# First MLP in five passes of 256 tokens and two of 512, in place of five of 288 and two of 432

## The chip, the cores and the metric

The program runs on one core of one Trainium2 chip, from one launch. The metric is the device time of one execution in microseconds. Each time that the kernel has is the median of several executions; beside them there is one execution under the hardware profiler, from which every row below is read.

## What is computed

Pooled attention over 4 batches, 8 heads, 576 positions of 64 channels, and then two MLPs over the 2304 tokens that come out of it, 512 channels wide. All inputs and outputs are float32.

```python
k_p = k.reshape(B, H, Sp, pool, D).mean(axis=3)          # pool = 8, Sp = 72
v_p = v.reshape(B, H, Sp, pool, D).mean(axis=3)
scores = scale * np.matmul(q, k_p.transpose(0, 1, 3, 2))
attn = softmax(scores)                                    # over the 72 pooled keys
x = np.matmul(attn, v_p) -> [2304, 512]

rms = np.sqrt(np.mean(x * x, axis=-1, keepdims=True) + 1e-06)
xn = x / rms * rms_g
g = xn @ w_gate                                           # 512 x 1536
silu = g * (1.0 / (1.0 + np.exp(-g)))
x = silu * (xn @ w_val) @ w_out                           # 1536 x 512

h = x @ w_in                                              # 512 x 2048
out = (h * (1.0 / (1.0 + np.exp(-h)))) @ w_out2           # 2048 x 512
```

The change concerns the first MLP alone, and how its tokens are cut.

## The kernel before

**Tokens.** Attention makes tokens in eight chunks of 288 (`CH`), two per batch; a chunk stands in the tile `xraw` as 128 partitions by 4 blocks of channels (`KT`) by 288 tokens. The first MLP runs over these chunks in passes. Passes 0 to 4 take chunks 0 to 4, one each (288 tokens). Chunks 5 to 7 are written to DRAM (`x_spill`) and read again for two wide passes of 432 tokens (`WB`). The name `CB` is the number of narrow passes.

**One step of a pass** treats one of the 12 blocks of 128 hidden channels (f = 0 to 11): `gate` and `val` multiply the pass's tokens by a block of w_gate and w_val, `down1` multiplies the product by a block of w_out into four accumulators. Each of the three is 12 matmuls on TensorE, since float32 is split in a high and a low part and three of the four products are taken (`mm3`, lines 261 to 263): 36 matmuls a step, whose moving operand is the pass's tokens, so 288 or 432 columns. Between them ScalarE does a tanh (L637), VectorE two products (L639, L655) and the split of the result in its two parts (ACT L241 or DVE L243 for the copy, L248 for the difference). The wide passes do the same in `gatew`, `valw`, `downw`.

**Weights** come from DRAM as float64 and are turned into two float32 parts by seven instructions a block (`w_block`: L175, L182 or L190, L194, and the two parts at L243/L241 and L248), mostly on VectorE. There are 36 such blocks. They are not all there when the first passes run: pass 0 does only f = 0 to 2 and pass 1 only f = 0 to 5 (`CUT`); what they leave out is done after pass 4, in two further passes that read the tokens back (`x_back`), pass 0 with 9 steps and pass 1 with 6. Pass 2 is the first with all 12 steps, and the first that needs every block. Steps before the end of pass 2: 3 + 6 + 12 = 21; after it 12 + 12 + 9 + 6 = 39; all times 36 matmuls are 2160 narrow matmuls. The wide passes have 2 x 12 x 36 = 864.

**Tokens for a pass** are split by `x_split` into the tiles `xT0` to `xT3`, one per block of channels, with one buffer each: a copy and a difference per tile, which may begin only when the last pass has read that tile for the last time.

**The second MLP** (line 786, `up2` and `down2`) is two levels of seven products in place of eight, in three blocks of 768 tokens, with moving operands of 384 and of 256 columns. Its code is not changed.

**The order** of all this is written out by hand as four strings of step names (`start`, `pair`, `last`, `second`), such as `2G0` for the next part of gate of step 0 of pass 2, `B17` for the next part of weight block 17, `:v` or `:g` or `:a` for the engine. `play` calls the parts in that order, and each engine takes its instructions in the order in which they were recorded. There is no other scheduler.

Of the kernel before, what the change touches and what calls it, by code (L numbers as in the profile page):

```python
# [22 lines left out]
def tile_pooled_attention_then_two_mlps(  # L23
# [25 lines left out]
    P = 128  # L49
# [21 lines left out]
    WB = (NCH - CB) * CH // 2  # L71
    WP = 448
# [201 lines left out]
    xraw = att.tile([P, KT, CH], F32, name="xraw")  # L274

# [304 lines left out]

    def x_spill(c, j):
        if c in x_d:
            nc.sync.dma_start(out=x_d[c][j], in_=xraw[:, j, :])
        else:
            for p, a, z in wide(c):
                n = p * WB - (c - CB) * CH
                nc.sync.dma_start(out=xw_d[p][j][:, a:z], in_=xraw[:, j, a + n:z + n])
        yield

    def wide(c):  # L590

        n = (c - CB) * CH
        for p in range(2):
            a, z = max(n, p * WB), min(n + CH, (p + 1) * WB)
            if a < z:
                yield p, a - p * WB, z - p * WB

    def steps(c):
# [7 lines left out]
            "r": lambda i: stats(c), "n": lambda i: normalise(c), "y": x_split,  # L606
# [16 lines left out]
    def gate(i, f):  # L623
        w = w_t["gate", f]
        pg = psum.tile([P, 512], F32, tag="up", bufs=2, name="pg")[:, :CH]
        for j in range(KT):
            m = slice(j * P, (j + 1) * P)
            mm3(pg, w[:, 0, m], w[:, 1, m], xT[j][:, 0, :CH], xT[j][:, 1, :CH], j == 0, j == KT - 1)
        yield
        if i == 0:  # L630

            g = early_x[:, f % 2 * CH:(f % 2 + 1) * CH]
            nc.vector.tensor_tensor(out=g, in0=pg, in1=early_x[:, 2 * CH:3 * CH], op=ALU.mult)
            yield
            pg = g
        th_t[i, f] = th = p1.tile([P, CH], F32, tag="ev", bufs=2, name="th")
# [4 lines left out]
        if i == 0:  # L641
            combine("g", th, th, early_x[:, 2 * CH:3 * CH], ALU.mult)
            yield

    def val(i, f):
        w = w_t["val", f]
        ps = psum.tile([P, 512], F32, tag="up", bufs=2, name="pv")[:, :CH]
        for j in range(KT):
            m = slice(j * P, (j + 1) * P)
            mm3(ps, w[:, 0, m], w[:, 1, m], xT[j][:, 0, :CH], xT[j][:, 1, :CH], j == 0, j == KT - 1)  # L650
# [6 lines left out]
        hT[i, f] = t = p1.tile([P, 2, CH], F32R, tag="hT", bufs=2, name="hT")  # L657
        yield from split(t[:, 0, :], t[:, 1, :], h, "v" if 2 <= i < NCH - 1 else "a", "v")

    def down1(i, f):  # L660
# [13 lines left out]
    def part_load(i):  # L674
        t = [slot() for _ in range(2)]
        part_t[i] = t = [t[e // 2][:, e % 2 * CH:(e % 2 + 1) * CH] for e in range(KT)]
# [4 lines left out]
    def y1_store(i, e):  # L681
# [4 lines left out]
        else:  # L686
            y = tmp("y")
# [7 lines left out]
    def x_back(i, j):  # L695
# [676 lines left out]
```

## Time and profile before

| what | value |
|---|---|
| median of 3 runs | 907.18 us (906.56 to 907.39) |
| the profiled execution | 906.69 us |
| its span, first to last instruction | 904.9 us |
| TensorE busy | 897.5 us |
| VectorE, ScalarE, GpSimd busy | 629.6, 541.0, 382.8 us |
| granted TensorE clock, mean | 0.998 |

A matmul's busy time in the profile reaches from its start to the modelled end of its results, and matmuls overlap; a busy TensorE is not one at its best rate. The rate is read from the starts of matmuls that follow each other. Busy times of the other engines are unions of their instructions' times.

Seen from TensorE, the span has five stretches: attention alone with filler matmuls up to 42 us; passes 0, 1 and 2 with attention for the next chunks and the weight blocks up to 166 us; passes 3 and 4 and the two left-over passes up to 384 us; the wide passes up to 556 us; and the second MLP. The windows in the rows below are cut close to these.

### The profile page before, as it was taken

How to read it: one execution, taken by the hardware profiler on the slowest of the kernel's cores; microseconds unless marked ns; L12 is line 12 of the kernel's file. 1: busy time of each engine (PE TensorE's matmuls, PEld its weight loads, DVE VectorE, ACT ScalarE, POOL GpSimd, SP SyncE). 2: the span in 40 equal slices, each digit the busy share in tenths (PEclk: the TensorE clock that was granted, in tenths of full speed). 3: DMA queues.
4: the chain of work that ended last, by engine and by line, in shares of the span. 5: the costliest groups of instructions: out<-in, count | busy, mean ns of one | idle time of the engine just before them, and what ended most of it. 6: DMA issues, size and time to landing. Idle time of an engine off the chain costs nothing.

```text
span 904.9 us, 17610 instructions
## 1 busy us (share of the span) xinstructions
PE 897.5 (99%) x6262; PEld 880.5 (97%) x6262; DVE 629.6 (70%) x1255; ACT 541.0 (60%) x1452; POOL 382.8 (42%) x488
## 2 busy tenths in 40 slices
PE   8999999999999999999999999999999999999998
PEld 8789999999999999999999999999999999999998
DVE  7899998665454836443477789757976589766675
ACT  6789876373354714344444556777657776577653
POOL 6646434372217521100028666980048810399100
PEclk9999999999999999999999999999999999999999
DMA  8765632351314322244468886266852678623485
GB/s 264 235 201 189 205 108 78 94 176 43 92 42 123 102 66 61 86 145 150 151 207 277 271 277 203 72 232 217 269 191 70 211 213 274 209 73 141 139 263 205
DMA packets 85260, 149.81 MB, mean 166 GB/s; under 512 B 8627, under 2 KB 53812, under 8 KB 85172
## 3 DMA queue, kind: packets, MB, share of 16 engines
q1 hardware_dynamic: 85172, 148.68, 50.8%
q8 instruction: 49, 0.80, 0.4%
q14 instruction: 39, 0.32, 0.1%
HBM read 116.21 MB, written 32.44 MB: 164 GB/s over the span
## 4 chain that ended last, share of the span: by engine, by line
PE 96%; POOL 1%; DMA 1%; issue 1%; ACT 1%; DVE 0%; SPq 0%; ACTq 0%; POOLq 0%
PE P L786 38%; PE pv L261 6%; PE pv L263 6%; PE pv L262 6%; PE pg L261 6%; PE acc L261 6%; PE acc L262 6%; PE pg L262 6%; PE acc L263 6%; PE pg L263 6%; PE sc L418 2%; PE pT L469 1%; DMA early_raw<-in_moe_w_gate_dram 1%; PE idle L331 1%; PE pv L504 1%
## 5 line engine op out<-in xcount | busy, mean ns | idle before, releaser
L786 PE MATMUL P<-xP,in 128*128 128x384 f32 x1008 | 176.5, 336 | 0.0
L786 PEld LDWEIGHTS P<-xP,in 128*128 128x128 f32 x1008 | 175.0, 188 | 0.1
L786 PE MATMUL P<-out,hc 128*128 128x256 f32 x1512 | 172.8, 276 | 0.0
L786 PEld LDWEIGHTS P<-out,hc 128*128 128x128 f32 x1512 | 172.6, 188 | 0.0
L248 POOL TENSOR_TENSOR in<-in,in 128x256 fp32r<-128x256 f32 x96 | 80.3, 845 | 112.1 <-DMA out_dram<-o 48.2
L241 ACT ACTIVATE hc<-h 128x384 fp32r<-128x384 f32 x144 | 73.6, 524 | 42.6 <-PE P L786 36.3
L248 DVE TENSOR_TENSOR hc<-h,hc 128x384 fp32r<-128x384 f32 x144 | 79.9, 581 | 18.5 <-ACT hc L241 15.1
L261 PE MATMUL pg<-xT,w_gate 128*128 128x288 f32 x240 | 72.6, 303 | 0.3 <-DVE hT L248 0.3
L261 PE MATMUL pv<-xT,w_val 128*128 128x288 f32 x240 | 72.8, 303 | 0.0
L261 PE MATMUL acc<-hT,w_out 128*128 128x288 f32 x240 | 72.2, 301 | 0.0
L263 PE MATMUL pv<-xT,w_val 128*128 128x288 f32 x240 | 70.9, 295 | 0.3 <-POOL w_val L248 0.3
L262 PE MATMUL acc<-hT,w_out 128*128 128x288 f32 x240 | 71.0, 296 | 0.0
L262 PE MATMUL pg<-xT,w_gate 128*128 128x288 f32 x240 | 70.9, 295 | 0.0
L262 PE MATMUL pv<-xT,w_val 128*128 128x288 f32 x240 | 70.8, 295 | 0.0
L263 PE MATMUL pg<-xT,w_gate 128*128 128x288 f32 x240 | 70.8, 295 | 0.0
L263 PE MATMUL acc<-hT,w_out 128*128 128x288 f32 x240 | 70.8, 295 | 0.0
L637 ACT ACTIVATE th<-pg 128x288 f32<-128x288 f32 x57 | 23.3, 409 | 70.0 <-PE pg L263 69.0
L436 ACT ACTIVATE pr<-sc,mx 96x72 f32<-96x72 f32 x192 | 57.9, 316 | 11.7 <-DVE mx L429 10.9
L248 POOL TENSOR_TENSOR in<-sums,in 128x256 fp32r<-128x256 f32 x72 | 58.5, 820 | 5.8 <-ACT in L241 5.5
L639 DVE SCALAR_TENSOR_TENSOR th<-th,pg 128x288 f32<-128x288 f32 x57 | 25.7, 451 | 36.8 <-ACT th L637 36.5
L263 PEld LDWEIGHTS pv<-xT,w_val 128*128 128x128 f32 x240 | 45.3, 189 | 0.6 <-POOL w_val L248 0.6
L261 PEld LDWEIGHTS pv<-xT,w_val 128*128 128x128 f32 x240 | 45.1, 188 | 0.7 <-ACT kbd L241 0.4
(236 smaller groups left out, 2324.1 us busy)
## 6 DMA issues: line engine op xcount, KB each, us to landing
out<-out SPq DMA_DIRECT2D x84, 512.0 KB, 4.6
out<-out2s SPq DMA_DIRECT2D x56, 256.0 KB, 2.9
in<-in SPq DMA_DIRECT2D x24, 512.0 KB, 3.7
raw<-in_moe_w_out_dram SPq DMA_DIRECT2D x18, 512.0 KB, 4.3
raw<-in_moe_w_in_dram SPq DMA_DIRECT2D x16, 512.0 KB, 3.7
early_raw<-in_moe_w_gate_dram SPq DMA_DIRECT2D x10, 512.0 KB, 4.4
early_raw<-in_moe_w_val_dram SPq DMA_DIRECT2D x10, 512.0 KB, 4.9
early_raw<-in_moe_w_out_dram SPq DMA_DIRECT2D x10, 512.0 KB
```

The source lines that it names most:

```text
L241: nc.scalar.activation(out=out, in_=in_, func=AF.Copy, scale=1.0 if scale is None else scale)
L248: ENGINES[engine[0] or usual].tensor_tensor(out=out, in0=in0, in1=in1, op=op)
L261: nc.tensor.matmul(ps, lhsT=whi, rhs=xhi, start=first, stop=False)
L262: nc.tensor.matmul(ps, lhsT=whi, rhs=xlo, start=False, stop=False)
L263: nc.tensor.matmul(ps, lhsT=wlo, rhs=xhi, start=False, stop=last)
L331: nc.tensor.matmul(idle[0][:, :P], lhsT=zero, rhs=zero, start=True, stop=True, skip_group_check=True)
L418: nc.tensor.matmul(ps[:TT, a * 2 * SP:(a + 1) * 2 * SP], lhsT=qT[:, a * TT:(a + 1) * TT], rhs=kbd[:, j, :], start=True, stop=True,)
L436: nc.scalar.activation(out=pr[:, a, e], in_=s4[:, a, e], func=AF.Exp, bias=mx[:, a, e:e + 1], accum_out=sm[:, a, e],)
L469: nc.tensor.transpose(ps[:n, a * TT:(a + 1) * TT], src, ident[:TT, :TT])
L637: nc.scalar.activation(out=th, in_=pg, func=AF.Tanh, scale=0.5)
L639: nc.vector.scalar_tensor_tensor(out=th, in0=th, scalar=1.0, in1=pg, op0=ALU.add, op1=ALU.mult)
L786: nc.tensor.matmul(ps, lhsT=a, rhs=b, start=first and n == 0, stop=n == 2, skip_group_check=True)
```

## The change

The narrow passes take 256 tokens (`TP`) in place of 288, still five of them, and the wide passes 512 in place of 432: 5 x 256 + 2 x 512 = 2304 as 5 x 288 + 2 x 432 was. Chunks of attention stay at 288 tokens. What chunk c has left over after pass c, 32 (c + 1) tokens, is copied by GpSimd into a new tile `left` and opens pass c + 1, so that pass c takes 32 c tokens from `left` and 256 - 32 c from `xraw`. `x_split` therefore has two copies and two differences per tile in passes 1 to 4 where it had one of each. For chunk 0 the left-over tokens are also scaled by GpSimd. Of chunk 4, 160 tokens go to the wide passes. The tiles in DRAM, the results and the loads for the second MLP are cut at the new places. Some tiles change their memory: the wide passes' `thw` stands where `hT` stood, `fr` has five places in place of six, `y1_wide` has one `e` buffer in place of two. The number of matmuls is the same, 140 filler matmuls included. The order strings are new throughout, for all engines.

```diff
-    WB = (NCH - CB) * CH // 2
-    WP = 448
+    TP = 256
+    WB = (NT - CB * TP) // 2
...
+    left = att.tile([P, KT, P], F32, name="left")
...
             nc.sync.dma_start(out=rs_d[c], in_=rs[:1])
             yield
+            t = kept(c)
+            combine("g", t, t, rs[:, None, TP:].to_broadcast([P, KT, CH - TP]), ALU.mult)
+            yield
             return
...
+    def kept(c):
+
+        n = (c + 1) * (CH - TP)
+        return left[:, :, P - n:] if c == 0 else left[:, :, :n]
+
     def x_spill(c, j):
         if c in x_d:
-            nc.sync.dma_start(out=x_d[c][j], in_=xraw[:, j, :])
+            n = c * (CH - TP)
+            if n:
+                nc.sync.dma_start(out=x_d[c][j][:, :n], in_=kept(c - 1)[:, j, :])
+            nc.sync.dma_start(out=x_d[c][j][:, n:], in_=xraw[:, j, :TP - n])
...
-    def x_split(j):
-        xT[j] = t = p1.tile([P, 2, CH], F32R, tag=f"xT{j}", bufs=1, name=f"xT{j}")
-        yield from split(t[:, 0, :], t[:, 1, :], xraw[:, j, :], "a", "v")
+    def x_tile(j):
+        if len(xT) == 2 and j not in xT:
+            p1.tile([P, 32], F32, tag="shift", bufs=1, name="shift")
+        xT[j] = t = p1.tile([P, 2, TP], F32R, tag=f"xT{j}", bufs=1, name=f"xT{j}")
+        return t
+
+    def x_split(c, j):
+        t = x_tile(j)
+        n = c * (CH - TP)
+        if n:
+            yield from split(t[:, 0, :n], t[:, 1, :n], kept(c - 1)[:, j, :], "a", "v")
+        yield from split(t[:, 0, n:], t[:, 1, n:], xraw[:, j, :TP - n], "a", "v")
+        if c < CB - 1:
+            copy("g", kept(c)[:, j, :], xraw[:, j, TP - n:])
+            yield
...
-        pg = psum.tile([P, 512], F32, tag="up", bufs=2, name="pg")[:, :CH]
+        pg = psum.tile([P, 512], F32, tag="up", bufs=2, name="pg")[:, :TP]
...
-            k = n_fr[0] % 6
+            k = n_fr[0] % 5
...
-        xw[j] = t = pw[0].tile([P, 2, WP], F32R, tag=f"x{j}", bufs=1, name=f"xw{j}")[:, :, :WB]
+        xw[j] = t = pw[0].tile([P, 2, WB], F32R, tag=f"x{j}", bufs=1, name=f"xw{j}")
...
-        thw[f] = th = pw[0].tile([P, WB], F32, tag="e", bufs=2, name="thw")
+        thw[f] = th = p1.tile([P, WB], F32, tag="hT", bufs=2, name="thw")
...
-        if p == 1 and e < 2:
-            y = pw[0].tile([P, WB], F32, tag="e", bufs=2, name="yw")
+        if e % 2:
+            y = pw[0].tile([P, WB], F32, tag="e", bufs=1, name="yw")
...
-        "B35 3n0 3y1:g 3y0 2H11 3n0 2H11:a 2D10 3y0:g 3y2 2H11 3y1 3n0 3y3 2D11 2D11 3y2 3y3 2D11 2D11"
+        "B35 3y1 3y1 2H11 2H11:a 3n0 3n0 3y1:g 2H11 3y0 3y0 3y0 2D10 3y0:g 3n0 3n0 3y2 3y2 3y2 3y1 3y3 3y3 3y0 "
+        "3y3 2D11 2D11 3y2 3y3 3y3 2D11 2D11"
```

How the instructions stand at the end of pass 2 and the start of pass 3. Names carry a number that tells buffers apart; `w_out11` is the last weight block, `hT` the split product for the last `down1`, `xT` the tokens of pass 3. VectorE before:

```order
L243 CAST w_out11_2322<-raw_2237 128x512
L248 TENSOR_TENSOR xraw_162<-xraw_162,rs_2304 128x288
L655 TENSOR_TENSOR pv_2308<-th_2299,pv_2308 128x288
...
L248 TENSOR_TENSOR hT_2332<-pv_2308,hT_2332 128x288
L248 TENSOR_TENSOR xT1_2326<-xraw_162,xT1_2326 128x288
...
L248 TENSOR_TENSOR xT2_2347<-xraw_162,xT2_2347 128x288
L248 TENSOR_TENSOR xT3_2352<-xraw_162,xT3_2352 128x288
L245 TENSOR_SCALAR y_2368<-acc1_1665 128x288
```

VectorE after, at the same place:

```order
L244 CAST w_out11_2355<-raw_2268 128x512
L249 TENSOR_TENSOR xT1_2358<-left_162,xT1_2358 128x96
L674 TENSOR_TENSOR pv_2333<-th_2346,pv_2333 128x256
L249 TENSOR_TENSOR xraw_161<-xraw_161,rs_2351 128x288 x2
L249 TENSOR_TENSOR hT_2362<-pv_2333,hT_2362 128x256
L249 TENSOR_TENSOR xT0_2368<-left_162,xT0_2368 128x96
L249 TENSOR_TENSOR xraw_161<-xraw_161,rs_2351 128x288 x2
L249 TENSOR_TENSOR xT2_2387<-left_162,xT2_2387 128x96
L249 TENSOR_TENSOR xT1_2358<-xraw_161,xT1_2358 128x160
L249 TENSOR_TENSOR xT3_2392<-left_162,xT3_2392 128x96
L249 TENSOR_TENSOR xT2_2387<-xraw_161,xT2_2387 128x160
L249 TENSOR_TENSOR xT3_2392<-xraw_161,xT3_2392 128x160
```

Four differences from `left` have come in between; the weight block and `hT` stand where they stood, and the operations of the step itself are 32 columns narrower.

GpSimd at the same place, before:

```order
L550 TENSOR_TENSOR ms_2261<-ms_2261,mhalf_122 96x3
L248 TENSOR_TENSOR w_val11_2281<-raw_2196,w_val11_2281 128x512
L248 TENSOR_TENSOR w_out11_2322<-raw_2237,w_out11_2322 128x512
L243 CAST xT1_2326<-xraw_162 128x288
L248 TENSOR_TENSOR xT0_2328<-xraw_162,xT0_2328 128x288
L338 TENSOR_TENSOR kv_2370<-kv_2370 96x256
```

And after:

```order
L552 TENSOR_TENSOR ms_2295<-ms_2295,mhalf_121 96x3
L249 TENSOR_TENSOR w_val11_2315<-raw_2230,w_val11_2315 128x512
L249 TENSOR_TENSOR w_out11_2355<-raw_2268,w_out11_2355 128x512
L244 CAST xT1_2358<-xraw_161 128x160
L249 TENSOR_TENSOR xT0_2368<-xraw_161,xT0_2368 128x160
L244 COPY left_162<-xraw_161 128x128 x2
L340 TENSOR_TENSOR kv_2414<-kv_2414 96x256
```

The copies of what chunk 3 leaves over stand behind the last weight blocks and ahead of the sums of v.

## Rows read from the trace of the kernel before

**Rows 1.** Page, parts 1 and 4: busy time; the chain that ended last.
```profile
PE 897.5 (99%) x6262; PEld 880.5 (97%) x6262; DVE 629.6 (70%) x1255; ACT 541.0 (60%) x1452; POOL 382.8 (42%) x488
...
PE 96%; POOL 1%; DMA 1%; issue 1%; ACT 1%; DVE 0%; SPq 0%; ACTq 0%; POOLq 0%
```

**Rows 2.** Windows: stretch, its length, then each engine's busy us and instructions.
```profile
core 0: us, PE busy (x) PEld busy (x) DVE busy (x) ACT busy (x) POOL busy (x), PEclk, DMA share, GB/s
...
40.00:105.00 65.00, 64.26 (x475) 60.49 (x474) 63.76 (x147) 58.10 (x170) 32.66 (x42) 1.00 0.61 192
105.00:165.00 60.00, 59.99 (x460) 59.64 (x459) 52.96 (x115) 40.35 (x90) 25.57 (x23) 1.00 0.33 107
165.00:384.00 219.00, 218.64 (x1688) 217.97 (x1688) 119.34 (x287) 98.29 (x366) 77.40 (x121) 1.00 0.29 87
384.00:552.00 168.00, 168.00 (x863) 161.11 (x862) 105.37 (x176) 83.95 (x163) 57.94 (x65) 1.00 0.64 214
```

**Rows 3.** Timeline of TensorE, narrow passes: start, us, engine, line, form.
```profile
379.81 0.29 PE L262 MATMUL pv<-xT,w_val 128*128 128x288 f32 x1
...
384.32 0.29 PE L263 MATMUL acc<-hT,w_out 128*128 128x288 f32 x1
```

**Rows 4.** The same view, wide passes and second MLP.
```profile
399.66 0.36 PE L261 MATMUL pv<-xw,w_val 128*128 128x432 f32 x1
...
403.57 0.36 PE L263 MATMUL acc<-hw,w_out 128*128 128x432 f32 x1
...
639.78 4.47 PE L786 MATMUL P<-out,hc 128*128 128x256 f32 x38
```

**Rows 5.** Page, part 5: a matmul of 256 columns, busy us, mean ns.
```profile
L786 PE MATMUL P<-out,hc 128*128 128x256 f32 x1512 | 172.8, 276 | 0.0
```

**Rows 6.** Timeline of VectorE, GpSimd and TensorE at the end of pass 2.
```profile
161.84 0.41 DVE L243 CAST w_out<-raw 128x512 fp32r<-128x512 f32 x1
163.05 0.46 DVE L655 TENSOR_TENSOR pv<-th,pv 128x288 f32<-128x288 f32 x1 [0.44 <-PE pv L263]
164.06 0.46 DVE L248 TENSOR_TENSOR hT<-pv,hT 128x288 fp32r<-128x288 f32 x1 [0.19 <-ACT hT L241]
...
162.33 1.32 POOL L248 TENSOR_TENSOR w_out<-raw,w_out 128x512 fp32r<-128x512 f32 x1 [2.26 <-DVE w_out L243]
...
164.44 0.29 PE L261 MATMUL acc<-hT,w_out 128*128 128x288 f32 x1
...
166.14 0.30 PE L261 MATMUL pg<-xT,w_gate 128*128 128x288 f32 x1
```

**Rows 7.** VectorE's waits, 40 to 105 us: waiter <- releaser: us, times, longest.
```profile
DVE th L639 <- ACT th L637: 0.6, 1, 0.6
DVE early_x L633 <- PE pg L263: 0.3, 1, 0.3
```

**Rows 8.** VectorE's waits, 105 to 165 us, the four longest.
```profile
DVE pv L655 <- PE pv L263: 1.9, 3, 0.8
DVE pT L243 <- PE pT L469: 1.4, 1, 1.4
DVE th L639 <- ACT th L637: 0.9, 1, 0.9
DVE raw L175 <- DMA raw<-in_moe_w_val_dram: 0.8, 1, 0.8
```

**Rows 9.** Groups by form, VectorE and GpSimd: count, busy us, mean ns of one.
```profile
L1049 DVE TENSOR_TENSOR o<-P,s 128x512 f32<-128x512 f32 x3 | 2.1, 687 | 0.4 <-PE P L786 0.4
L1049 DVE TENSOR_TENSOR o<-P,s 128x256 f32<-128x256 f32 x3 | 1.2, 415 | 0.0
L248 DVE TENSOR_TENSOR vt<-vs,vt 32x64 fp32r<-32x64 f32 x1 | 0.2, 215 | 0.0
L248 DVE TENSOR_TENSOR vbd<-vs,vbd 64x64 fp32r<-64x64 f32 x8 | 2.3, 289 | 0.2
L243 POOL COPY rest<-pr 96x144 f32<-96x144 f32 x15 | 6.7, 452 | 25.8 <-DVE pr L248 25.5
```

More of the change, by code (lines that the diff above doesn't have):

```diff
@@ L579, in normalise @@
             yield
+    def kept(c):
+        n = (c + 1) * (CH - TP)
+        return left[:, :, P - n:] if c == 0 else left[:, :, :n]
     def x_spill(c, j):
         if c in x_d:
-            nc.sync.dma_start(out=x_d[c][j], in_=xraw[:, j, :])
-        else:
-            for p, a, z in wide(c):
-                n = p * WB - (c - CB) * CH
-                nc.sync.dma_start(out=xw_d[p][j][:, a:z], in_=xraw[:, j, a + n:z + n])
-        yield
[L590 to L596, printed above, removed]
+            n = c * (CH - TP)
+            if n:
+                nc.sync.dma_start(out=x_d[c][j][:, :n], in_=kept(c - 1)[:, j, :])
+            nc.sync.dma_start(out=x_d[c][j][:, n:], in_=xraw[:, j, :TP - n])
+        else:
+            n = c * CH - CB * TP
+            for p in range(2):
+                a, z = max(n, p * WB), min(n + CH, (p + 1) * WB)
+                if a < z:
+                    nc.sync.dma_start(out=xw_d[p][j][:, a - p * WB:z - p * WB], in_=xraw[:, j, a - n:z - n])
+        yield
     def steps(c):
@@ L675, in part_load @@
         t = [slot() for _ in range(2)]
-        part_t[i] = t = [t[e // 2][:, e % 2 * CH:(e % 2 + 1) * CH] for e in range(KT)]
+        part_t[i] = t = [t[e // 2][:, e % 2 * TP:(e % 2 + 1) * TP] for e in range(KT)]
         for e in range(KT):
@@ L722, in fr @@
         if not late:
-            k = n_fr[0] % 6
+            k = n_fr[0] % 5
             n_fr[0] += 1
-            return p1.tile(
-                [P, 2, 256], F32R, tag="hT" if k > 3 else f"xT{k}", bufs=2 if k > 3 else 1, name=name
-            )
+            pool, tag = (pw[0], "e") if k > 3 else (p1, f"xT{k}")
+            return pool.tile([P, 2, 256], F32R, tag=tag, bufs=1, name=name)
         n_late[0] += 1
@@ L850, in y1_wide @@
         yield
-        for c in range(CB, NCH):
-            for q, a, z in wide(c):
-                if q == p:
-                    n = p * WB - (c - CB) * CH
-                    nc.sync.dma_start(out=y1_d[c][:, e, a + n:z + n], in_=y[:, a:z])
+        nc.sync.dma_start(out=y1_d[CB + p][:, e, :], in_=y)
         yield
@@ L864, in x2_steps @@
         t0 = c * N2
-        for n in range(t0 // CH, (t0 + N2 - 1) // CH + 1):
-            a, z = max(t0, n * CH), min(t0 + N2, (n + 1) * CH)
-            nc.sync.dma_start(out=x2raw[:, :, a - t0:z - t0], in_=y1_d[n][:, :, a - n * CH:z - n * CH])
+        for (n, m), y1 in zip(parts, y1_d):
+            a, z = max(t0, n), min(t0 + N2, n + m)
+            if a < z:
+                nc.sync.dma_start(out=x2raw[:, :, a - t0:z - t0], in_=y1[:, :, a - n:z - n])
         yield
```

39 lines of the change are left out of this document (20 added, 19 removed), and 324 rows, old and new, of tables (last, pair, second, start).

## The prediction

> **What bounds the kernel now.** I read the page first: TensorE is busy for 897.5 us of the span of 904.9 us, and the chain that ended last lies on it for 96% [rows 1]. So the first question is what a matmul costs, and the second where TensorE is only just fed. For the cost I took the starts of matmuls that follow each other without a break. In the narrow passes 35 matmuls start between 379.81 and 384.32 us [rows 3]: 4.51 / 34 = 132.6 ns each for 288 columns. In the wide passes 21 start between 399.66 and 403.57 us: 3.91 / 20 = 195.5 ns for 432 columns. In the second MLP 38 matmuls of 256 columns take 4.47 us together [rows 4]; less the 276 ns of the last one [rows 5], 4.19 / 37 = 113.4 ns. At the higher of the clock's two levels, 2.4 GHz, which the granted clock of 1.00 is [rows 2], columns alone would be 106.7, 120.0 and 180.0 ns. So 256 columns carry 6.7 ns on top, 288 carry 12.6 and 432 carry 15.5: between 256 and 288 there is a step of 5.9 ns beyond the 13.3 ns of the columns.
>
> Then I read the windows by stretch, to see who else is full [rows 2]. From 40 to 105 us VectorE is busy 63.76 of 65 us, from 105 to 165 us 52.96 of 60: it has 1.24 + 7.04 = 8.3 us to spare in 125. From 165 us on it is busy 54 to 63% and TensorE alone sets the pace. The end of pass 2 shows what the first stretch means [rows 6]: the high part of the last weight block is made at 161.84 us on VectorE, its low part ends at 162.33 + 1.32 = 163.65 us on GpSimd, the last hT ends at 164.06 + 0.46 = 164.52 us, and TensorE begins the `down1` that needs both at 164.44. Nothing lies ready there. Up to the start of pass 3 at 166.14 us, TensorE and VectorE end together.
>
> **The matmuls.** The change takes 32 columns off 2160 matmuls and adds 80 to 864; the sum of columns is the same, so only the step counts. A narrow one goes from 132.6 to 113.4 ns, if 256 columns cost in the first MLP what they cost in the second: 19.2 ns less. For 512 columns there is no row. Twice the row of 256 is 226.8 ns; 195.5 plus 80 columns at 2.4 GHz (33.3 ns) is 228.8; with one more step of 5.9 ns it is 234.7. I take 228.8, since 432 columns already carry more than 288 do and 2 x 256 would want a lower overhead than the nearest row has; both ends stay for the range. The wide passes then cost 864 x 33.3 ns = +28.8 us (27.0 to 33.9). VectorE and ScalarE get longer there too, but VectorE was busy 105.37 of 168 us [rows 2], and TensorE gets more time than they do, so I cost that at nothing. The cover would be gone if a step's products took longer than its 36 matmuls, now 8.2 us.
>
> The narrow side falls in two parts. After pass 2 there are 39 steps of 36, 1404 matmuls: 1404 x 19.2 = -27.0 us. VectorE has 99.7 us to spare of 219 there, ScalarE and GpSimd more, so all of it should reach the end. Before that there are 21 steps, 756 matmuls, which would be -14.5 us, if TensorE were alone.
>
> **The first 166 us.** It is not alone. I went through VectorE's instructions up to the last weight block in both orders. The weight work, the attention work and their places are the same but for exchanges of equal size. 71 operations of the steps get narrower by 32 columns, at (687 - 415) / 256 = 1.06 ns a column [rows 9] 34 ns each, -2.4 us; 12 differences of `x_split` lose 64 columns on average, -0.8 us; 8 new differences from `left` come in, 32 or 64 columns wide, between 215 and 289 ns by the nearest rows [rows 9], 250 taken, +2.0 us. That is -1.2 us in all; for the start of pass 3, four more of 96 columns, some 300 ns each, bring it back to about 0. VectorE's work ahead of pass 3 is thus the same, and TensorE's is 14.5 us less; so pass 3 starts earlier only by what VectorE's own waits shrink. Its waits for TensorE, and for the tanh that follows a matmul, are 0.6 + 0.3 us in the first window [rows 7] and 1.9 + 1.4 + 0.9 in the second [rows 8]: 5.1 us. Those can go when TensorE gets there early; what waits for a DMA or for ScalarE's weight work stays. I take -5.1 us for this stretch, with 0 and the whole 8.3 as ends. The other 9.4 us of the 14.5 become TensorE waiting for weights and hT.
>
> **The small parts.** GpSimd gets 16 copies into `left`, near 0.45 us each by the copy of 144 columns [rows 9], 7.2 us; it is idle for half of the first 165 us. Behind them on its queue stand sums of v and scores' weights, and the next chunk's writes of `xraw` now wait for these copies; they come several microseconds later. The starts of passes 1 to 4 have eight short operations more on ScalarE and VectorE together for each pair of tiles, and TensorE's work that covers them has shrunk by a seventh. In passes 1 and 2 this is in VectorE's sum; at passes 3 and 4 TensorE may wait: 0 to 1 us each, +1.0 taken for both. The DMA issues on SP go from 451 to 449. The changed buffers of the wide passes (`thw` beside the results) are read while up to four products lie in PSUM, so I cost them at nothing.
>
> **The sum.** -5.1 - 27.0 + 28.8 + 1.0 = -2.3 us against the profiled execution of 906.69 us, of which 904.9 are the span: 904.4. The median of the runs is 0.5 us above that execution, so 904.9 us.
>
> **A rule against it.** The rows give 256 columns 113.4 ns and 288 columns 132.6. The Trainium skill, "TensorE: Matmul & The Clock Gate", section "Back-to-back issue gap", has the gap between isolated matmuls as the columns at 2.4 GHz plus about 2.5 ns, one constant for every width. By that rule the re-cut changes nothing on TensorE as a whole, 2160 x 13.3 = 28.7 us off and 28.8 us on. The trace doesn't agree with the constant, which is 6.7 to 15.5 ns in its rows, nor with its being the same.
>
> **The rivals.**
> (a) *VectorE does not hold TensorE*, since operations that can be late are in truth moved behind the urgent ones: the whole 14.5 us arrive, and the sum is -14.5 - 27.0 + 28.8 + 1.0 = -11.7, 895.5 us. For it: the order is new throughout, and the exchanges were weighed only by their sums. Against it: VectorE's work ahead of the weight blocks has not become less.
> (b) *The first stretch gives nothing.* VectorE's waits only move, because each of its products now waits for a matmul that itself waited for a weight block: 0 - 27.0 + 28.8 + 1.0 = +2.8, 910.0 us. The point is 2.8 us: if fewer of the 8.3 idle microseconds vanish, the kernel is not faster at all; fewer than 1.0, and it is measurably slower. For it: only 1.24 us are idle until 105 us. Against it: most of the later idle time has TensorE as its cause.
> (c) *Narrow matmuls lose only their columns*, 13.3 ns, because the 6.7 ns on top belong to the second MLP and not to 256 columns: 119.3 ns, 1404 x 13.3 = -18.7, and -5.1 - 18.7 + 28.8 + 1.0 = +6.0, 913.2 us. It turns to the slower side from 115.0 ns on. Against it: the row has the same shapes and types. The constant gap of the Trainium skill would give the same.
> (d) *512 columns are dear*, 234.7 ns: -5.1 - 27.0 + 33.9 + 1.0 = +2.8, 910.0 us. It decides from 231.5 ns on.
>
> **How the numbers follow.** The forecast has 0.46, (a) 0.14, (b) 0.18, (c) 0.08, (d) 0.07, mixtures of these 0.07. A measurement of this kernel tells about 0.2%, 1.8 us, from no change. The forecast's own ends are -8.3 - 27.0 + 27.0 = -8.3 (898.9 us) and, with 1.5 us less won and 1.0 more at the passes' starts, about +0.2 (907.4 us); some 0.30 of its 0.46 lie over 1.8 us below, 0.12 within, 0.04 above. With (a) and part of the mixtures faster is 0.47; with a quarter of (b) and a third of (d) within is 0.21; slower is 0.32, most of it (b) and (c). Cases of both signs hold much of the chance. The range reaches from 898 us, which leaves out most of (a), to 912 us, which holds (b) and (d) and leaves out (c): one in ten on either side.
>
> **What would show it.** In the profile of the changed kernel: starts of narrow matmuls 113 to 114 ns apart and of wide ones near 229; pass 3 beginning near 161 us with VectorE busy over 95% from 105 us to there and TensorE waiting for VectorE or GpSimd some 9 us in all before it; passes 3 to the end of the left-over ones 26 us shorter than 218, with TensorE without breaks; the wide stretch 29 us longer. Narrow matmuls at 119 ns, or pass 3 before 154 us or after 165 us, would each mean that a step of the sum is wrong. The forecast also fails if the waits before pass 3 are long enough to bring the granted clock down to its lower level, which in the trace of before it held at 1.00 from 40 us on.

## The result, and the profile after

The changed kernel is slower: 913.14 us median (911.69 to 917.17), against 907.28 us for the kernel before on the same chip, a ratio of 1.0064 with a 95% interval of 1.0041 to 1.0088. The forecast was 904.9 us with a range of 898 to 912. The profiled execution took 912.81 us, of which 911.0 are the span.

The page of the changed kernel, parts 1 and 4, as [rows 1] of before:

```profile
PE 897.7 (99%) x6262; PEld 848.9 (93%) x6262; DVE 621.4 (68%) x1272; ACT 541.3 (59%) x1468; POOL 380.3 (42%) x504
...
PE 86%; DVE 6%; DMA 3%; POOL 2%; ACT 2%; issue 1%; SPq 0%; ACTq 0%; POOLq 0%; DVEq 0%
```

TensorE's busy time is the same within 0.2 us although about half of its work was recut, and the chain that ended last now leaves TensorE for 14% of the span where it left it for 4%.

To place the difference I cut both spans at the same five events: the first gate matmul, the first of pass 3, the first of the wide passes, the first of the second MLP, the end. Windows of the changed kernel (stretch, length, then busy us and instructions of each engine, granted clock, DMA share, GB/s; the first gate matmul is at 43.22, pass 2 begins at 101.54):

```profile
43.22:161.54 118.32, 114.53 (x931) 109.73 (x931) 111.30 (x265) 96.40 (x261) 55.81 (x71) 1.00 0.49 154
...
101.54:161.54 60.00, 58.50 (x493) 57.57 (x492) 54.80 (x132) 43.79 (x102) 24.62 (x25) 1.00 0.34 106
161.54:359.65 198.11, 196.96 (x1687) 196.23 (x1685) 111.16 (x289) 94.91 (x369) 76.11 (x124) 1.00 0.32 97
359.65:556.29 196.64, 196.41 (x853) 160.10 (x853) 110.60 (x178) 88.70 (x166) 56.53 (x65) 1.00 0.55 188
556.29:911.02 354.73, 350.99 (x2533) 350.05 (x2531) 255.48 (x471) 231.41 (x531) 160.53 (x192) 1.00 0.54 182
```

And of the kernel before, cut at the same events:

```profile
42.23:166.14 123.91, 123.16 (x929) 119.81 (x926) 115.60 (x257) 96.83 (x250) 59.08 (x65) 1.00 0.48 151
...
101.74:166.14 64.40, 64.39 (x494) 64.04 (x492) 57.33 (x125) 43.36 (x95) 27.08 (x24) 1.00 0.31 100
166.14:384.45 218.31, 217.95 (x1683) 217.28 (x1682) 118.33 (x284) 97.72 (x365) 76.34 (x120) 1.00 0.29 87
384.45:551.61 167.16, 167.16 (x857) 160.27 (x856) 104.89 (x174) 83.95 (x163) 57.82 (x65) 1.00 0.64 214
551.61:904.91 353.30, 349.50 (x2533) 349.12 (x2531) 257.55 (x473) 232.62 (x533) 161.19 (x192) 1.00 0.56 184
```

| stretch | before | after | predicted | measured |
|---|---|---|---|---|
| start to first gate matmul | 42.23 | 43.22 | 0 | +1.0 |
| first gate matmul to pass 3 | 123.91 | 118.32 | -5.1 | -5.6 |
| pass 3 to the wide passes | 218.31 | 198.11 | -26.0 | **-20.2** |
| wide passes | 167.16 | 196.64 | +28.8 | +29.5 |
| second MLP | 353.30 | 354.73 | 0 | +1.4 |
| sum | | | -2.3 | +6.1 |

The first row can't be put down to the change: one and the same kernel, profiled twice (the one with tiles at 160 below), had its first gate matmul at 40.93 and at 45.07 us.

One row carries most of it: the stretch in which TensorE alone sets the pace gave 5.8 us less than forecast. The timeline of TensorE shows why. In pass 3 (start, us, engine, line, form) 36 matmuls follow each other without a break between

```profile
163.51 0.28 PE L264 MATMUL pv<-xT,w_val 128*128 128x256 f32 x1
...
167.71 0.28 PE L264 MATMUL acc<-hT,w_out 128*128 128x256 f32 x1
```

which is 4.20 / 36 = 116.7 ns each, not the 113.4 of [rows 4]. Over all 2001 narrow matmuls that another of the same width follows without a wait, the mean from start to start is 117.3 ns; before it was 132.5. In the second MLP of the same execution 256 columns still cost what they did: 46 of them

```profile
639.83 5.38 PE L804 MATMUL P<-out,hc 128*128 128x256 f32 x46
```

less 0.28 for the last are 5.10 / 45 = 113.3 ns. The wide matmuls are about where they were put: 27 intervals between

```profile
400.10 0.39 PE L264 MATMUL pg<-xw,w_gate 128*128 128x512 f32 x1
...
406.32 0.39 PE L264 MATMUL acc<-hw,w_out 128*128 128x512 f32 x1
```

are 6.22 / 27 = 230.4 ns; the mean of all is 230.1.

The end of pass 2 answers to [rows 6]. VectorE, GpSimd and TensorE:

```profile
157.88 0.43 DVE L244 CAST w_out<-raw 128x512 fp32r<-128x512 f32 x1
159.62 0.42 DVE L249 TENSOR_TENSOR hT<-pv,hT 128x256 fp32r<-128x256 f32 x1
...
158.44 1.31 POOL L249 TENSOR_TENSOR w_out<-raw,w_out 128x512 fp32r<-128x512 f32 x1 [1.93 <-issue]
...
160.13 0.28 PE L262 MATMUL acc<-hT,w_out 128*128 128x256 f32 x1
...
161.54 0.28 PE L262 MATMUL pg<-xT,w_gate 128*128 128x256 f32 x1
```

The last low part ends at 159.75, the last hT at 160.04, and TensorE takes both at 160.13: the same meeting as before, 4.3 us earlier. Pass 3 begins at 161.54 where the forecast had it near 161.

So two questions were left. Why do 256 columns cost 117.3 ns in the first MLP and 113.4 in the second? And is it VectorE that holds the first stretch?

### The profile page after: what moved, and what is told of

The parts are those of the page before. It is cut to its first block, busy times and chain, and to the rows that moved or that the text cites. A ratio compares the mean times of both kernels' runs of the same rounds, so it can differ in the third digit from the quotient of the medians.

```text
span 911.0 us, 17654 instructions
## 1 busy us (share of the span) xinstructions
PE 897.7 (99%) x6262; PEld 848.9 (93%) x6262; DVE 621.4 (68%) x1272; ACT 541.3 (59%) x1468; POOL 380.3 (42%) x504
## 4 chain that ended last, share of the span: by engine, by line
PE 86%; DVE 6%; DMA 3%; POOL 2%; ACT 2%; issue 1%; SPq 0%; ACTq 0%; POOLq 0%; DVEq 0%
PE P L804 38%; PE pv L262 5%; PE pv L263 5%; PE pv L264 5%; PE pg L262 5%; PE pg L263 5%; PE pg L264 5%; PE acc L263 4%; PE acc L264 4%; PE acc L262 4%; PE sc L420 2%; PE idle L333 1%; PE pT L471 1%; DMA kv<-in_k_dram 1%; DMA early_raw<-in_moe_w_gate_dram 1%
## 5 line engine op out<-in xcount | busy, mean ns | idle before, releaser
L262 PE MATMUL pv<-xT,w_val 128*128 128x256 f32 x240 | 69.5, 290 | 2.4 <-DVE hT L249 1.4
L262 PE MATMUL pg<-xT,w_gate 128*128 128x256 f32 x240 | 68.9, 287 | 0.5 <-DVE ms L548 0.4
L262 PE MATMUL acc<-hT,w_out 128*128 128x256 f32 x240 | 68.7, 286 | 0.0
L263 PE MATMUL pg<-xT,w_gate 128*128 128x256 f32 x240 | 67.3, 280 | 0.4 <-DVE xT L249 0.4
L263 PE MATMUL acc<-hT,w_out 128*128 128x256 f32 x240 | 67.4, 281 | 0.0
L264 PE MATMUL pv<-xT,w_val 128*128 128x256 f32 x240 | 67.1, 280 | 0.1
L263 PE MATMUL pv<-xT,w_val 128*128 128x256 f32 x240 | 67.1, 280 | 0.0
L264 PE MATMUL acc<-hT,w_out 128*128 128x256 f32 x240 | 67.0, 279 | 0.0
L264 PE MATMUL pg<-xT,w_gate 128*128 128x256 f32 x240 | 67.0, 279 | 0.0
L656 ACT ACTIVATE th<-pg 128x256 f32<-128x256 f32 x57 | 22.0, 386 | 60.5 <-PE pg L264 58.6
L249 POOL TENSOR_TENSOR sums<-out 128x256 f32<-128x256 f32 x8 | 7.7, 960 | 104.4 <-DVE out L195 95.6
L262 PEld LDWEIGHTS pv<-xT,w_val 128*128 128x128 f32 x240 | 45.2, 188 | 4.0 <-DVE hT L249 2.3
L262 PEld LDWEIGHTS pg<-xT,w_gate 128*128 128x128 f32 x240 | 45.2, 188 | 1.1 <-DVE hT L249 0.7
```

The source lines that it names most:

```text
L249: ENGINES[engine[0] or usual].tensor_tensor(out=out, in0=in0, in1=in1, op=op)
L262: nc.tensor.matmul(ps, lhsT=whi, rhs=xhi, start=first, stop=False)
L263: nc.tensor.matmul(ps, lhsT=whi, rhs=xlo, start=False, stop=False)
L264: nc.tensor.matmul(ps, lhsT=wlo, rhs=xhi, start=False, stop=last)
L656: nc.scalar.activation(out=th, in_=pg, func=AF.Tanh, scale=0.5)
```

## Experiments

**The place of the narrow tiles.** A tile's start within a partition can be read from the built kernel. Taken modulo 256 bytes, hT, xT2 and xT3 of the changed kernel begin at 32, xT0 and xT1 at 160, all stationary tiles of the first MLP at 224; in the second MLP the moving tiles begin at 224 and the stationary ones at 32 or 160. The changed kernel's pad of 128 bytes between two of the xT tiles makes that pattern. In the kernel before, all narrow tiles begin at 160, and the stationary ones at 224 as well: the change itself moved hT, xT2 and xT3. (Whether 256 bytes is the period of what follows was not tried.) Three kernels differ from it only in where the pads stand. At 224:

```diff
-        if len(xT) == 2 and j not in xT:
-            p1.tile([P, 32], F32, tag="shift", bufs=1, name="shift")
+        if not xT:
+            p1.tile([P, 16], F32, tag="shift", bufs=1, name="shift")
...
         hT[i, f] = t = p1.tile([P, 2, TP], F32R, tag="hT", bufs=2, name="hT")
+        if len(hT) == 1 and not fill:
+            fill.append(p1.tile([P, 16], F32, tag="fill", bufs=1, name="fill"))
```

> Edit: in the changed kernel only, the pad that stands between two of the narrow tiles is moved, so that all narrow tiles (xT0 to xT3 and hT) begin at 224 modulo 256 bytes of a partition; the moving tiles of the second MLP, whose matmuls start 113.4 ns apart, begin there too. In the changed kernel hT, xT2 and xT3 begin at 32, xT0 and xT1 at 160, and the first MLP's matmuls start some 117.5 ns apart. Theory A (the address of the moving tile sets the price): narrow matmuls 113.4 ns, 1404 x 4.1 = -5.8 us after pass 3 has begun; 907 us. Theory B (the price belongs to the stage: to its weights, its three matmuls on one accumulator, or to what the other engines do at the time): 117 to 118 ns as before, 913 us. The wide tiles keep their addresses: their matmuls stay at 230 ns in both.

At 160 there is no pad in front and one of 32 behind:

> The same edit with all narrow tiles at 160 modulo 256. Theory A: matmuls on xT0 and xT1 stay at the 114 to 116 ns that they take in the changed kernel, those on xT2, xT3 and hT come down to that from 117 to 118: some 115 ns for all, 1404 x 2.5 = -3.5 us, 909.6 us. Theory B: 117 to 118 ns, 913 us.

At 32 there is one of 32 in front and none behind:

> The same edit with all narrow tiles at 32 modulo 256. Theory A: matmuls on xT0 and xT1 go up to the 118 ns of the others, 118 for all: about +0.7 us after pass 3 has begun, 914 us. Theory B: no change in any tile, 913 us, and xT0 and xT1 stay 2 to 4 ns cheaper than xT2 and xT3.

Measured: 915.85 us with the tiles at 224 (ratio 1.0091, 1.0064 to 1.0117), 909.69 at 160 (1.0022, 0.9995 to 1.0048), 915.00 at 32 (1.0079, 1.0052 to 1.0106). The timeline of TensorE in pass 3, 36 intervals each. At 160:

```profile
162.08 0.28 PE L262 MATMUL pg<-xT,w_gate 128*128 128x256 f32 x1
...
166.16 0.28 PE L262 MATMUL pg<-xT,w_gate 128*128 128x256 f32 x1
```

At 224:

```profile
162.06 0.28 PE L264 MATMUL pv<-xT,w_val 128*128 128x256 f32 x1
...
166.38 0.28 PE L264 MATMUL acc<-hT,w_out 128*128 128x256 f32 x1
```

That is 4.08 / 36 = 113.3 ns against 4.32 / 36 = 120.0 for the same instructions in the same order. Over all narrow matmuls the means are 114.7 ns at 160, 117.2 at 32 and 119.6 at 224. Theory B falls: the price does not belong to the stage. Theory A is right that the tile's place sets it, and right on 160 and on 32, where xT0 and xT1 rose from 116.7 and 115.6 to 117.3 and 117.2. It is wrong on 224: what is cheap in the second MLP is the dearest place in the first. So the moving tile's own start does not set the price alone.

The windows from pass 3 to the wide passes follow. At 160:

```profile
99.28:158.68 59.40, 57.66 (x493) 56.74 (x492) 54.55 (x131) 43.62 (x102) 24.55 (x25) 1.00 0.37 109
158.68:353.70 195.02, 193.55 (x1686) 192.66 (x1684) 111.89 (x289) 94.68 (x369) 75.85 (x124) 1.00 0.32 98
```

At 224:

```profile
100.03:160.02 59.99, 59.19 (x493) 58.46 (x492) 54.93 (x132) 43.92 (x102) 24.62 (x25) 1.00 0.35 105
160.02:360.73 200.71, 200.17 (x1686) 199.65 (x1685) 112.27 (x288) 94.85 (x368) 76.02 (x124) 1.00 0.31 96
```

From pass 3 to the wide passes the difference is 5.7 us for 1404 x 4.9 = 6.9 us of matmuls. In pass 2 (the first row of each) the same edit takes 432 x 4.9 = 2.1 us from TensorE and the pass becomes 0.6 us shorter: there, TensorE is not what counts.

**More places, and the wide tiles.** With a longer pad in front (48 words, none behind) the narrow tiles stand at 96, and the wide ones 64 bytes further on:

> Edit: in the changed kernel, all narrow tiles at 96 modulo 256, and since the pad that this takes is 64 bytes longer, the wide tiles at 96 (hw, xw0, xw1) and 224 (xw2, xw3) in place of 32 and 160; the second MLP's tiles move 64 bytes too. So far narrow matmuls cost 114.7 ns at 160, 117.2 at 32, 119.6 at 224. Theory A (the price is a smooth function of the start modulo 256 with its low point near 128): 114 to 115 ns, and from the start of pass 3 to the wide passes 194 to 195.5 us, as with 160. Theory A2 (160 is a place of its own): 117 ns or more and 198 us or more. For the wide tiles: if 512 columns follow the same curve, hw, xw0 and xw1 fall from 229.3 to some 227 and xw2, xw3 rise from 231.6 to some 236; if not, all stay at 229 to 232.

Measured 925.00 us (1.0187, 1.0157 to 1.0217). Narrow matmuls 119.1 ns and 200.6 us to the wide passes: theory A2. The wide ones follow no curve that I had written down: hw, xw0 and xw1 rose to 232.6, xw2 and xw3 fell to 229.4. What made the kernel so slow stood elsewhere: the second MLP took 362.6 us in place of 354.7, its 256-column matmuls 119.1 ns. Its stationary tiles hc lie in the memory of the wide tiles and had moved with them.

Halfway between 160 and 224:

> Edit: in the changed kernel, all narrow tiles at 192 modulo 256, halfway between 160 (114.7 ns) and 224 (119.6 ns); wide tiles unmoved. Theory H with a smooth curve between its points: 117 ns, from pass 3 to the wide passes 198 us. If only the exact difference of 192 from the stationary tiles is cheap: 119 ns or more, 200 us or more. If the conflict needs an exact difference of 0 or 128: 114.7 ns or less, 195 us or less.

118.3 ns and 199.6 us, so the price is high already 32 bytes from the cheap place, between the first two of the three cases; the time was 916.29 us (1.0077, 1.0042 to 1.0112).

Then the wide tiles, all at one place, with the narrow ones left at 160. At 96 there are two short pads:

```diff
             pw.append(ctx.enter_context(tc.tile_pool(name="pw", bufs=1, reuse_waits="tile")))
+            pw[0].tile([P, 16], F32, tag="shift", bufs=1, name="shift")
...
-        if (p, j) == (0, 2):
-            pw[0].tile([P, 32], F32, tag="shift", bufs=1, name="shift")
+        if (p, j) == (0, 3):
+            pw[0].tile([P, 16], F32, tag="fill", bufs=1, name="fill")
```

> Edit: narrow tiles at 160 modulo 256 as before in this study, and all wide tiles (hw, xw0 to xw3) at 96 in place of 32 and 160. Theory E (512 columns follow the start as 256 do): another mean than 230.1 ns, by up to 4 ns either way, 3.5 us of the wide stretch of 196.6 us. Theory F (512 columns do not): 229.5 to 230.5 ns, 196.6 us.

> The same with all wide tiles at 160 modulo 256, where 256 columns are cheapest. Theory E: 226 to 228 ns in all tiles, the wide stretch 194 us or less in place of 196.6. Theory F: 230 ns and 196.6 us; xw2 and xw3, which stand at 160 already, cost 230.7 and 232.5 and speak for F.

> Edit: narrow tiles at 160 modulo 256, all wide tiles at 32; with them the second MLP's stationary tiles hc, which take the same memory, all begin at 32. So far the price of 256 columns reads as follows, in the first MLP (stationary tiles all at 224, moving at 32, 96, 160, 224): 117.2, 119.1, 114.7, 119.6 ns; in the second (moving all at 224; stationary at 32 and 160 mixed, all at 96, all at 160): 113.6, 118.7, 117.8 ns. Theory H (the price goes by the start of the moving tile less that of the stationary one, modulo 256: 0 gives 119.6, 64 gives 117 to 118, 128 gives 119, 192 gives 114.7): the difference is 192 in the second MLP here, so its 256-column matmuls start 114 to 115 ns apart and its length stays within 2 us of the 354.4 us that it has with the mixture. Theory I (only the mixture of two starts is cheap in the second MLP): 117 ns or more, and 4 us or more on top. The wide matmuls, at 32 alone: 229.3 ns if each tile keeps the price that it has in the mixture (196.0 us for the stretch), about 233 if all tiles at one place are dear as at 96 and at 160 (199 us).

| wide tiles and hc at | 512 columns, ns | wide stretch, us | second MLP, 256 columns, ns | second MLP, us | time, us |
|---|---|---|---|---|---|
| 32 and 160 (as changed) | 230.1 | 196.6 | 113.6 | 354.4 | 909.69 |
| 96 | 233.3 | 199.4 | 118.7 | 364.0 | 922.50 |
| 160 | 233.3 | 199.4 | 117.8 | 359.9 | 917.80 |
| 32 | 229.0 | 195.7 | 116.3 | 360.3 | 913.43 |

The stretches come from one profiled execution each. The times are medians of 10, 2, 3 and 7 runs, beside which the kernel before took 907.94, 908.55, 908.55 and 909.16 us. The length of the second MLP holds its 1008 matmuls of 384 columns too, whose tiles moved as well: 174.4, 176.0, 173.6 and 176.4 ns, from the first row to the last.

Theory E is right that 512 columns depend on the place, by up to 4.3 ns, and wrong on the direction: 160 is dear for them. Theory F falls. The timeline of the second MLP with hc at 160 alone, beside [rows 4]:

```profile
639.77 5.46 PE L804 MATMUL P<-out,hc 128*128 128x256 f32 x45
```

(5.46 - 0.28) / 44 = 117.7 ns for what cost 113.4, with the moving tiles unmoved: the stationary tile's place counts as much. Theory H, a price by the difference of the two starts, asked for 114 to 115 ns with hc at 32; 116.3 were measured, between it and theory I. Both fall as written. The wide matmuls at 32 alone took 229.0 ns, near the 229.3 that stood for each tile keeping its price. What holds is narrower: at one width and one order of instructions, the places of the two operands move the price of 256 columns between 113.4 and 120 ns, and a mixture of two starts in the stationary tiles was cheaper than either alone. The rule behind it stays open.

**Does VectorE hold the first stretch?** Two of the seven operations of each weight block are halved, in the changed kernel and in the one before; both leave out the other half of the block.

```diff
         low, _ = w_words(kind, f)
+        if kind != "in2":
+            low = low[:, :256]
...
         low, up = w_words(kind, f)
+        if out is None:
+            low, up = low[:, :256], up[:, :256]
```

> Edit: in the changed kernel the two integer operations of every block of first-MLP weights on VectorE (the shift of the low words and the join) take 256 of their 512 columns, which leaves the other half of each block of weights wrong. By the rows of the changed kernel (434 and 695 ns for 512 columns) that takes some 0.2 + 0.35 us from VectorE for each of 28 blocks between 42 and 160 us, 15 us in all. Theory C (VectorE holds TensorE until pass 3, as the prediction has it): pass 3, which begins at 161.5 us, begins 4 to 7 us earlier, at 154.5 to 157.5, and the time falls by as much, to 906 to 909 us. Theory D (something else holds it there: transfers, the order, ScalarE): pass 3 begins less than 1.5 us earlier and the time stays within 2 us of 913.

> Edit: in the kernel before, the two integer operations of every first-MLP weight block on VectorE take 256 of their 512 columns, which leaves half of each block of weights wrong; the same edit in the changed kernel brought pass 3 forward by 3.7 us, counted from the first gate matmul (114.6 us in place of 118.3). Theory C (in the kernel before TensorE and VectorE end together, and the change has made VectorE the later one): from the first gate matmul to pass 3 121.5 us or more in place of 123.9, a gain of at most 2.4 us. Theory G (VectorE alone holds pass 3 in both kernels): a gain of 3.5 us or more, 120.4 us or less.

Windows from the first gate matmul to pass 3, the changed kernel halved, then the kernel before halved:

```profile
42.41:157.03 114.62, 112.86 (x931) 109.21 (x931) 102.12 (x265) 95.66 (x261) 50.45 (x71) 1.00 0.51 159
```

```profile
42.97:165.35 122.38, 121.95 (x928) 119.61 (x926) 103.23 (x253) 96.00 (x249) 52.89 (x64) 1.00 0.48 152
```

The changed kernel gains 118.3 - 114.6 = 3.7 us for 9.2 us less of VectorE's busy time (15 were expected), the one before 123.9 - 122.4 = 1.5 us for 12.4 us less. In the first, pass 3 began at 157.0 us, 4.5 earlier in its span, and the time was 909.11 us (against the kernel before 1.0004, 0.9980 to 1.0028), in the second 907.04 us (one run). Theory C stands in both, for the first at its low end or, counted from the event, just under it: the runs fit two engines that end together before the change, and a VectorE that ends later after it. It isn't the whole: with the changed kernel's blocks halved TensorE is still idle for 1.8 us.

**Relief by GpSimd.** If VectorE's amount of work holds the stretch, ten low parts moved to GpSimd should give some of it back (narrow tiles at 160):

```diff
-        "1y2 1y3 1y3 H2 H2 3m1 2s2 B14 1G0 2V3 1H0 2w1 B8:v 1G0 1G0 B9 1H0 1G1 B10 B14 D2 2p1 B11 2w3 B11 1H0 "
+        "1y2 1y3 1y3 H2 H2 3m1 2s2 B14 1G0 2V3 1H0 2w1 B8 1G0 1G0 B9 1H0 1G1 B10 B14 D2 2p1 B11 2w3 B11 1H0 "
```

and so for the other nine.

> Edit: in the changed kernel with all narrow tiles at 160 modulo 256, the low parts of ten weight blocks (8, 9, 14, 15, 17, 22, 23, 24, 25, 27) are made by GpSimd and not by VectorE: ten instructions of some 0.7 us off VectorE, ten of 1.3 us on GpSimd, which is idle for half of that stretch. The step from the first gate matmul to pass 3 takes 117.7 us without this, and TensorE stands for some 7 us in it. Theory C (VectorE's amount of work holds TensorE there): 2 to 4 us less, 113.7 to 115.7 us, and the time 2 to 4 us less than the 909.7 us without it, 906 to 908. Theory J (single late products hold it, each behind something else in VectorE's order, and not the amount): less than 1 us gained. Theory K (GpSimd's longer instructions make the blocks late): slower by 1 us or more, with TensorE waiting for GpSimd's w tiles.

Measured 909.76 us (1.0011, 0.9981 to 1.0041): no gain in the time, and the stretch became longer.

```profile
41.38:161.58 120.20, 114.03 (x932) 108.64 (x931) 111.65 (x257) 96.44 (x261) 73.24 (x82) 1.00 0.49 152
```

Without it:

```profile
40.93:158.68 117.75, 113.47 (x931) 108.29 (x931) 112.02 (x267) 96.20 (x261) 57.64 (x72) 1.00 0.51 156
```

VectorE has ten instructions fewer, and is busy for 111.65 us in place of 112.02: of some seven microseconds that were to go, 0.4 went. (TensorE's idle time without the relief is 4.3 us by this row, not the 7 of the expectation.) The groups by form over the same stretch (count, busy us, mean ns) show which instructions grew. With the relief:

```profile
L195 DVE SCALAR_TENSOR_TENSOR early_raw<-early_raw 128x512 uint32<-128x512 uint32 x26 | 20.2, 791 | 0.9 <-ACT early_raw L191 0.8
...
L183 DVE TENSOR_SCALAR early_raw<-early_raw 128x512 uint8<-128x512 uint8 x8 | 7.1, 882 | 0.0
```

Without it:

```profile
L195 DVE SCALAR_TENSOR_TENSOR early_raw<-early_raw 128x512 uint32<-128x512 uint32 x26 | 17.7, 697 | 0.0
...
L183 DVE TENSOR_SCALAR early_raw<-early_raw 128x512 uint8<-128x512 uint8 x8 | 6.5, 811 | 0.0
```

The means hide that few instructions grew, and by much. Of the 26 joins (L195) 23 take 0.65 to 0.86 us, and three take 1.24, 1.46 and 1.81. One of the three, with the GpSimd instruction beside it, and the same join without the relief:

```profile
101.21 1.75 POOL L249 TENSOR_TENSOR w_out<-early_raw,w_out 128x512 fp32r<-128x512 f32 x1
102.04 1.46 DVE L195 SCALAR_TENSOR_TENSOR early_raw<-early_raw 128x512 uint32<-128x512 uint32 x1
```

```profile
101.06 0.68 DVE L195 SCALAR_TENSOR_TENSOR early_raw<-early_raw 128x512 uint32<-128x512 uint32 x1
```

Each of the three began well inside a low part that GpSimd was making, and each ended 0.55 us after that low part did. No join without the relief began so. Over the whole stretch ten instructions of VectorE took 0.25 us or more beyond the median of their form, 7.4 us in all, against five and 2.5 us without the relief; every one of them began inside a GpSimd instruction and ended 0.1 to 0.6 us after it. By these ends such an instruction does not run a little slower throughout, it stands until GpSimd's is over. The Trainium skill, "GPSIMD Engine Reference", section "Specifications", says that GpSimd's way to the on-chip memory is shared with VectorE; this trace agrees, with these numbers.

VectorE's idle time grew as well, from 5.7 to 8.6 us. In pass 2 it waits for transfers:

```profile
DVE early_raw L176 <- DMA early_raw<-in_moe_w_val_dram: 1.6, 1, 1.6
DVE raw L176 <- DMA raw<-in_moe_w_val_dram: 1.4, 1, 1.4
```

Without the relief these two were 0.4 and 1.0 us. And TensorE waited 1.0 us once for vbd of GpSimd, which it had not done. Theory K has the sign for the stretch, not for the time, and its reason is not there: TensorE's weight loads wait 0.2 us for a w tile of GpSimd, 0.3 without the relief. Theory J's "less than 1 us gained" is met, and C's 2 to 4 us are not; yet the run doesn't part the two, since VectorE's busy time fell by only 0.4 us: the edit did not take the load away that it was meant to take. What it shows is that moving these ten low parts does not relieve VectorE.

**The cheaper place again.** The kernel with the narrow tiles at 160, more often:

> The changed kernel with all narrow tiles at 160 modulo 256, unchanged, with more rounds, since its first interval against the kernel before (0.9995 to 1.0048) left open whether the cut into 256 and 512 gains once the tiles stand at the cheaper place. Added up from the stretches of the profiles, it is 1.2 us shorter ahead of pass 3, 23.3 us less in the passes after it, of which the first MLP's wide passes give back 29.5 and the second MLP 1.1, while the first stretch counted from the first gate matmul gains 6.2: +1.1 us in all. Theory L (the sum of stretches is right): ratio 1.000 to 1.003. Theory M (the prediction's sum with 113.4 ns, -2.3 us, would hold with the cheaper tiles): ratio 0.996 to 0.999.

909.04 us against 907.45, ratio 1.0019 (1.0002 to 1.0037): theory L. With its tiles at 160 the re-cut is still 0.2% slower, by the interval at most 0.4%, and not faster.

## Why the prediction was wrong, step by step

**The first 166 us** came near the number, -5.6 us from the first gate matmul for -5.1 forecast, pass 3 at 161.54 where "near 161" stood, but by another way than the forecast's. It had VectorE's work ahead of pass 3 unchanged and its waits 5.1 us shorter. By the two windows above VectorE's busy time fell by 4.3 us, from 115.60 to 111.30, and its idle time by only 1.3, from 8.3 to 7.0. The waits for TensorE and the tanh did go, from 5.1 us to 1.0; those for transfers, ScalarE and GpSimd, which the forecast left as they were, grew from 2.2 to 5.5 us. Three rows of pass 2 after the change:

```profile
DVE raw L176 <- DMA raw<-in_moe_w_val_dram: 1.0, 1, 1.0
DVE sq L249 <- POOL sq L249: 0.7, 1, 0.7
DVE th L658 <- ACT th L656: 0.5, 2, 0.3
```

Of the busy time, 2.6 us are the narrower operations of the steps (2.4 forecast), and 1.4 us are stalls beside GpSimd, as in the relief above: 4.0 us before the change, 2.6 after; the rest is not traced. That the sum came out right is luck. VectorE was also not over 95% busy from 105 us on; in pass 2 it was 54.8 of 60 us. And TensorE stood idle for 3.8 of 118.3 us, where some 9 were forecast; 756 matmuls had become cheaper by 15.2 ns, 11.5 us, not by 14.5, so 5.9 us of what TensorE saved did not arrive. The waits that the profile lists for TensorE there are, but for 0.4 us behind its own scores, for VectorE's products and not for weights: hT 1.4 us, th 0.9, xT and ms 0.4 each. The first of them:

```profile
PE pv L262 <- DVE hT L249: 1.4, 3, 0.9
```

That VectorE holds TensorE is what these and the halved operations speak for; whether by its amount of work or by single products that stand behind something else was not parted.

**The step that failed** is the first half of the matmuls' price: "A narrow one goes from 132.6 to 113.4 ns, if 256 columns cost in the first MLP what they cost in the second". They cost 117.3 as the tiles lie: 1404 x (132.5 - 117.3) = -21.3 us instead of -27.0, and with 1.1 us of stalls -20.2. The row was the right one for shape and type, as the text against rival (c) says; what it did not hold still was the place of the two tiles. The change's own pad was part of it: it took most narrow tiles from 160, where they stood for the 132.5 ns, and the prediction cost no change of place. With the tiles at 160 again the same order gives 114.7 ns and a stretch of 195.0 us, 23.3 us less than before and 3.1 of the missing 5.8. Of the other 2.7, some 2.0 are the price, 17.8 ns saved and not 19.2, and the rest is waiting.

**512 columns** were well sized: 33.3 ns more forecast, 230.1 - 195.6 = 34.5 measured, +29.5 us for +28.8. Rival (d) needed 231.5 ns to decide, which the layouts with 233.3 reach.

**The small parts.** The starts of passes were put at +1.0; after pass 3 began TensorE waits for 1.3 us: 0.5 behind GpSimd's sum of v, and 0.8 where the wide passes begin, as these rows of TensorE's waits from pass 3 on show:

```profile
PE pv L262 <- ACT xw L242: 0.6, 1, 0.6
PE pT L471 <- POOL kv L340: 0.5, 1, 0.5
PE pv L263 <- DVE xw L249: 0.2, 1, 0.2
```

The first and the last I had at nothing. The second MLP, not changed, cost +1.4 us: 12 of the wide matmuls run between its own, before as after, 0.4 us, its 384-column matmuls take 174.4 ns in place of 173.8, 0.6 us, and its 256-column ones 0.4 us more.

**The rivals.** (c) gave 913.2 us, and 913.1 came. Its number was met by luck and its reason was not: the narrow matmuls cost 117.3 ns and not its 119.3, and the second MLP and the late first gate matmul, at nothing in its sum, made up for that. Nor do the 6.7 ns on top of the columns belong to the second MLP: at 160 the first has 8.0 on average. The constant gap of the Trainium skill, "TensorE: Matmul & The Clock Gate", section "Back-to-back issue gap", which the page gives for isolated matmuls, doesn't fit these streams: at one width the gap over the columns goes from 6.7 to 13.3 ns here with the tiles' places. (a) is out, pass 3 began at 161.5 and not before 154. (b) is out by the first stretch.

With 117.3 ns in place of 113.4 the prediction's own sum is -5.1 - 21.3 + 28.8 + 1.0 = +3.4, 910.6 us: the other side of no change, and still inside the range. The measured parts are -5.6 - 20.2 + 29.5 + 1.4 + 1.0 = +6.1 on the span of 904.9, 911.0 us; the second MLP and the first gate matmul, both put at nothing, carried it over the end. The range was too narrow because the 113.4 ns carried no bound of their own, though the 19.2 ns saved hung on one row from another stage; a bound at the 119.3 of rival (c) would have put +8 us into the forecast's own range.

## What to carry to other kernels

The price of a matmul of one width is a property of where its two tiles lie as well as of its columns: take it from a row with the same tiles, or give it the spread that the profile's rows of neighbouring widths show, and when a recut moves tiles, cost every later stage that shares their memory. Work saved on an engine that another one holds arrives only up to that one's slack. Here the sum for it came out within half a microsecond, yet the holder's work fell where it was put at the same, and its other waits grew: cost both, and check both. Work moved from VectorE to GpSimd is not off VectorE's bill: look for instructions of VectorE that end just after one of GpSimd's.

## What the runs showed of the hardware that I had not expected

- **Operand places.** 256 columns took 114.7 to 119.6 ns on average in the first MLP and 113.6 to 119.1 in the second, and 512 columns 229.0 to 233.3, with nothing changed but the starts of the tiles, by multiples of 32 bytes. One layout moved by 64 bytes cost 8 us in a stage that the change does not touch.
- **VectorE beside GpSimd.** A join of 512 columns, 0.68 us as a rule, took 1.24 to 1.81 us when it began inside a low part on GpSimd, and ended 0.55 us after that. So the mean rose from 697 to 791 ns with ten more GpSimd instructions in the stretch.
- **The granted clock near the start.** With TensorE busy without a break, it stayed at 1.00, the higher of its two levels, from 30 to 50 us in one execution, and was granted 0.85 and 0.80 on average in another of the same instructions up to there. From 10 to 20 us TensorE had been busy for 9.11 us in the one and 7.97 in the other, and from 20 to 30 us without a break at 1.00 in both; what decides, these rows don't show. Windows of the kernel with narrow tiles at 160, then of the one with the wide tiles at 32:

```profile
30.00:40.00 10.00, 10.00 (x68) 7.29 (x67) 8.70 (x20) 7.39 (x28) 6.60 (x10) 1.00 0.81 260
40.00:50.00 10.00, 10.00 (x71) 8.07 (x72) 9.88 (x25) 9.18 (x20) 5.39 (x7) 1.00 0.47 142
```

```profile
30.00:40.00 10.00, 10.00 (x59) 7.67 (x58) 8.82 (x17) 6.72 (x24) 7.01 (x13) 0.85 0.83 264
40.00:50.00 10.00, 10.00 (x58) 8.09 (x56) 7.65 (x21) 7.25 (x23) 4.11 (x6) 0.80 0.24 78
```

The first gate matmul stood at 40.93 us in the one and at 45.70 in the other. The spans of the ten runs of the kernel at 160 go with their mean granted clock: 904.7 to 905.3 us at 1.000, 907.2 and 908.0 at 0.997, 911.8 at 0.994, 914.6 at 0.990. That is why the stretches above are counted from an event and not from the start, and why a difference of 2 us between kernels needs many runs.
